# One batch boundary regrouped in a fused attention and mixer kernel: token products, transposes and one output tile in another order, q and k loaded one pair later

## The chip, the cores and the metric

The kernel runs on one core of one Trainium2 chip. The metric is device time in microseconds (us) of one execution; smaller is better. The kernel before has a median of 386.81 us over 4 runs (386.44 to 387.4).

## The reference

There are 8 batches of 12 heads, with 448 positions and a head dimension of 64. Cosine attention comes first: q and k are divided by their row norms, the scores are scaled by 1/tau, a softmax is taken, and the weights multiply v. The heads are joined to x of 448 by 768 for each batch. A mixer follows: one product along the tokens (448 to 256 and back), one along the channels (768 to 1536 and back), each with a ReLU between its two halves and a residual sum.

```python
q_n = q / (norm(q, axis=-1) + 1e-6);  k_n = k / (norm(k, axis=-1) + 1e-6)
attn = softmax(matmul(q_n, k_n.T) / tau)
x = matmul(attn, v)                                   # joined over heads: B, 448, 768
h = maximum(x.T @ w_tok1, 0.0) @ w_tok2
u = x + h.T
out = u + maximum(u @ w_ch1, 0.0) @ w_ch2
```

## The kernel before, in words

The work is cut into 48 pairs of heads, six to a batch; pair i belongs to batch i // 6. The order of all instructions is written out by hand: each engine runs its own queue in the order in which the source issues to it, and semaphores join the queues.

A pair passes through these steps, each a function of the source:

- `load_qk` and `load_v` (L121 and below) issue the loads on SyncE (SP). The q and k buffers hold 7 pairs, the v buffers 4.
- `square` (L237 on GpSimd, L235 on ScalarE) squares q and k, `sums` (L253, VectorE) adds them over the head dimension, `norms` (L264 and L265) takes the root on ScalarE as a logarithm and an exponential, and with `dve=True` (L261 and L262) adds the epsilon and inverts on VectorE. `scaled` (L276, GpSimd) multiplies q and k by the result. `tpose` (L300) turns both on TensorE, and VectorE copies them to `qk` (L302).
- `score(i, c)` (L323) makes the scores of a quarter of the keys in a two-bank PSUM tile, and ScalarE writes their exponentials to `pt` (L324). There are four quarters, c = 0 to 3.
- `pv` (L362) or `pv_wide` (L380) multiply them with v, and VectorE divides by the row sums (L365 and L366, or L383 and L384) to give `x`. `pv` takes two one-bank tiles, one a head; `pv_wide` takes one two-bank tile for both heads.
- `tok1` (L393, copy with ReLU L396) and `tok2` (L407, sum L410) are the token product; they give `u16`. `udma` (L416) turns `u16` into `ut` by a DMA transpose on SP. `upose` (L423, copy L424) does it on TensorE instead.

The channel product of a batch comes as a queue of units: 12 of `m_ch1` (`psG`, L433; ReLU L436 on ScalarE) and then those of `m_ch2` (`psF`, L449; sum L453 on VectorE). `refill(0)` fills the queue for batch 0 while pair 7 is in the main loop; a unit is taken out between the steps of a pair.

PSUM is split in two pools that rotate. Pool "b" has 2 buffers of one bank, pool "s" has 3 buffers of two banks. A new tile of "s" waits until the third tile before it is read out; a new one of "b" waits for the second before it. Scores and units called with `wide=True` take "s"; `tpose`, `tok1`, `tok2`, `upose` and `pv` take "b"; `pv_wide` takes "s".

Pairs 0 to 5 are staged in a first stretch without units. The end of batch 0 is written out around two iterations. In iteration i = 6 (`NPAIR`) TensorE is given the last two score quarters of pair 6, `tpose(7)`, `tok1(5)` and `tok2(4)`. In iteration i = 7 it is given three score quarters of pair 7, `tok2(5)`, `upose` of pairs 3 and 4 together, `upose` of pair 5, `pv` of pair 6, the first unit (`psG` number 0), the last score quarter of pair 7, `tpose(8)`, the second unit, `tok1(6)`, and then the scores of pair 8. Pairs 0, 1 and 2 were turned by DMA (`ut` parts 0, 1, 2).

On SP the loads of q and k of pair i + 6 are issued in iteration i. Each DMA on SP waits, before its issue, for the landing of the eighth DMA before it. From pair 12 on the keys' last 64 rows come as separate small loads (`kr`).

Of the kernel before, what the change touches and what calls it, by code (L numbers as in the profile page):

```python
# [22 lines left out]
def kernel(  # L23
# [20 lines left out]
    DT = D // 128  # L44
# [4 lines left out]
    NP_ALL = B * NPAIR  # L49
# [4 lines left out]
    DMA_T0 = 16  # L54
# [37 lines left out]
    pipe = {}  # L92
# [4 lines left out]
    def old(i):  # L97
        return i < OLD
# [22 lines left out]
    def load_qk(i):  # L121
        b, h0 = i // NPAIR, 2 * (i % NPAIR)
        n = i // HP
        half.setdefault(n, {})
        st = pipe[i] = {}
        st["q"] = qkv.tile([SC, QS, E], FP32, name=f"qf_{i}", tag="qf")
        nc.sync.dma_start(out=st["q"][:].rearrange("p (g c) e -> p g (c e)", g=2),
                          in_=q[b, h0:h0 + 2].rearrange("g (p c) e -> p g (c e)", c=NCH))
        st["k"] = load_rows(i, "k", k[b], 7)
        if not old(i) and "kr" not in half[n]:  # L130
            half[n]["kr"] = load_rest(i, "k", k[b])
# [107 lines left out]
    def squares(i):  # L239
        square(i, 0)  # L240
        square(i, 1)
# [45 lines left out]
    def scaled(i):  # L287
        scale(i, 0)
        scale(i, 1)
# [80 lines left out]
    def pv_wide(i):  # L370
        st = pipe[i]
        vt = vts[(i // HP) % NV]
        st["x"] = att.tile([128, 4, 128], FP16, name=f"x_{i}", tag="x", bufs=3)
        psO = ps2.tile([128, 2, 512], FP32, name=f"psO_{i}", tag="s")
        o = psO[:, :, 0:4 * (E + 2)].rearrange("p h (m e) -> p h m e", m=4)
        for hh in range(2):
            for m, lo in enumerate(windows(i // NPAIR)):
                for c in range(NCH):
                    at = (2 * c + hh) * S + lo
                    nc.tensor.matmul(o[:, hh, m, 0:E + 1], pts[i % 2][0:SC, at:at + 128],  # L380
                                     vt[0:SC, i % HP, NCH * hh + c, 0:E + 1], start=(c == 0), stop=(c == NCH - 1))
        rec = att.tile([128, 2, 4], FP32, name=f"rec_{i}", tag="rec2", bufs=2)
        nc.vector.reciprocal(out=rec[:], in_=o[:, :, :, E])  # L383
        nc.vector.tensor_tensor(out=st["x"][:].rearrange("p m (h e) -> p h m e", h=2), in0=o[:, :, :, 0:E],  # L384
                                in1=_bcast_free(rec[:], E), op=ALU.mult)
# [40 lines left out]
    def m_ch1(b, ct, wide):  # L426
        if b // 2 not in gts:
            gts[b // 2] = mix.tile([128, CT, 2 * S], FP16, name=f"gt_{b // 2}", tag="gt", bufs=1)
        gt = gts[b // 2]
        lo = 64 * (b % 2)  # L430
        psG = (ps2 if wide else ps).tile([128, 512], FP32, name=f"psG_{b}_{ct}", tag="s" if wide else "b")
        for dt in range(DT):
            nc.tensor.matmul(psG[:, 0:S], wc1t[:, dt, ct * 128:(ct + 1) * 128],  # L433
                             ut[b][:, dt].rearrange("p m s -> p (m s)")[:, lo:lo + S],
                             start=(dt == 0), stop=(dt == DT - 1))
        nc.scalar.activation(out=gt[:, ct, (b % 2) * S:(b % 2 + 1) * S], in_=psG[:, 0:S], func=AF.Relu)  # L436

    ost = {}
# [77 lines left out]
    with tc.manual_schedule():  # L516
        for i in range(3):
            load_qk(i)
        load_v(0)
        load_qk(3)  # L520
        load_v(1)
        load_qk(4)
        load_v(2)
        load_qk(5)
        load_v(3)
        nc.scalar.add_instruction(mybir.InstLoadActFuncSet(
            name=nc.get_next_instruction_name(), act_func_set_id=ACT_SET_LN_EXP,
            ins=[], outs=[]))
        weights_tok1()

        square(0, 1, act=True)
        square(0, 0, act=True)
        sums(0, 1, 2)
        norms(0, 1, 2)
        sums(0, 0, 1)
        norms(0, 1, 2, dve=True)
        norms(0, 0, 1)
        scale(0, 1, nc.vector)
        norms(0, 0, 1, dve=True)
        scale(0, 0)  # L540
        square(1, 1, act=True)
        square(1, 0, act=True)
        square(2, 1, act=True)
        warm(40, True)
        sums(1)
        norms(1)
        tpose(0, 1, 2)
        warm(3, True)
        tpose(0, 0, 1)
        warm(5, True)  # L550
        square(2, 0)
        weights_tok2()
        score(0, 0)
        score(0, 1)
        norms(1, dve=True)
        scale(1, 0)
        scale(1, 1, nc.vector)
        sums(2)
        norms(2)
        cast_v(0)  # L560
        score(0, 2)
        warm(8)
        tpose(1)
        score(0, 3)
        warm(6)
        norms(2, dve=True)
        square(3, 1, act=True)
        square(3, 0)
        load_v(4)
        load_qk(6)  # L570

        for i in range(1, NPAIR):
            if i == 1:
                scale(2, 0)
                scale(2, 1, nc.vector)
            else:
                scaled(i + 1)
                if i != 3:
                    weights_ch1(max(i - 3, 0))
            load_qk(i + 6)  # L580
            score(i, 0)
            score(i, 1)
            sums(i + 2)
            norms(i + 2)
            if i >= 2:
                tok1(i - 2)
            pv_wide(i - 1)
            norms(i + 2, dve=True)
            cast_v(i)
            square(i + 3, 0)  # L590
            if i == 1:
                warm(10)
            score(i, 2)
            score(i, 3)
            tpose(i + 1)
            if i >= 2:
                tok2(i - 2, pe=True)
            square(i + 3, 1, act=True)
            if i == 1:
                place_w2()  # L600
            load_v(i + 4)
            if 2 <= i < NPAIR - 1:
                udma(i - 2)

        i = NPAIR
        load_qk(i + 6)
        scaled(i + 1)
        score(i, 0)
        score(i, 1)
        sums(i + 2)  # L610
        norms(i + 2)
        tok1(i - 2)
        pv_wide(i - 1)
        norms(i + 2, dve=True)
        cast_v(i)
        load_v(i + 4)
        squares(i + 3)
        scaled(i + 2)
        weights_ch1(3)
        score(i, 2)  # L620
        score(i, 3)
        tpose(i + 1)
        tok1(i - 1)
        tok2(i - 2, pe=True)

        def side(i):
            if i + 6 < NP_ALL and i + 2 < DMA_T0:
                load_qk(i + 6)  # L630
            cast_v(i)
            if i + 3 < NP_ALL:
                squares(i + 3)
            if i in (8, 11):
                weights_ch2((i - 8) // 3)
            if i + 2 < NP_ALL:
                norms(i + 2)
                norms(i + 2, dve=True)
                scaled(i + 2)
                if i + 2 >= DMA_T0:  # L640
                    tpose_dma(i + 2)
            if i + 6 < NP_ALL and i + 2 >= DMA_T0:
                load_qk(i + 6)
            if i + 4 < NP_ALL:
                load_v(i + 4)

        for i in range(NPAIR + 1, NP_ALL):
            b, pj = i // NPAIR, i % NPAIR
            for c in range(KC):
                score(i, c)  # L650
            if i == NPAIR + 1:
                tok2(i - 2, pe=True)
                upose(i - 4, 2)
                upose(i - 2)
                sums(i + 2)
            pv_rest(i - 1)
            pv(i - 1, 0)
            pv(i - 1, 1)
            if i == NPAIR + 1:
                refill(0)  # L660
            elif pj == 2 and b > 1:
                refill(b - 1)
            side(i)
            fed[0] += fed[1]
            unit(True)
            if old(i):
                score(i, KC)
            else:
                score_rest(i)
            if i > NPAIR + 1:  # L670
                tok2(i - 2)
            if i + 1 < DMA_T0:
                tpose(i + 1)
            if due():
                unit(True)
            while due():
                unit()
            tok1(i - 1)
            if i + 3 < NP_ALL:
                sums(i + 3)  # L680
        last = NP_ALL - 1
        unit(True)
        pv_rest(last)
        pv(last, 0)
        pv(last, 1)
        unit(True)
        tok2(last - 1)
        unit(True)
        tok1(last)
        unit(True)  # L690
        unit(True)
        tok2(last)
        refill(B - 1)
        while queue:
            unit()
# [35 lines left out]
```

## Time and profile before

| what | value |
|---|---|
| median of 4 runs | 386.81 us (386.44 to 387.4) |
| the profiled execution's own time | 386.58 us |
| span inside it | 384.8 us |
| mean granted TensorE clock | 0.99 |
| TensorE matmuls busy | 372.3 us, 97% of the span |
| TensorE weight loads busy | 243.4 us, 63% |
| VectorE busy | 217.5 us, 57% |
| ScalarE busy | 226.6 us, 59% |
| GpSimd busy | 238.0 us, 62% |
| DMA | 64.21 MB, mean 167 GB/s |

The span is what the profile shows of the execution; the own time also holds what lies around it. PE is TensorE, PEld its weight loads, DVE VectorE, ACT ScalarE, POOL GpSimd, SPq the issues on SyncE. A timeline row has the start, the duration of the merged group, the engine, the line, the operation, and in brackets the idle time before it with what ended it. Ends of matmuls are modelled, so two groups on PE overlap a little in the rows.

### The profile page before, as it was taken

Reading aid. Unit: us, or ns where it says so; the run is one execution under the profiler, and the core shown is the slowest. Engines: PE = TensorE matmul, PEld = TensorE weight load, DVE = VectorE, ACT = ScalarE, POOL = GpSimd, SP = SyncE. Lnnn points to the kernel's source line nnn. Section 1 sums busy time; section 2 is a strip of 40 time slices with the busy share of each in tenths; the row PEclk is TensorE's granted clock in tenths of the full one; section 3 lists DMA queues with packets and bytes.
Section 4 is the critical chain, followed back from the end, with each engine's and each line's share of the span. In section 5 each row is a group of like instructions: output and inputs, shape, how many; then the busy total and the mean of one; then the engine's idle time right before and its main releaser. Section 6 shows DMA issues by size and latency. Waiting matters only on the chain.

```text
span 384.8 us, 10226 instructions
## 1 busy us (share of the span) xinstructions
PE 372.3 (97%) x4124; PEld 243.4 (63%) x4124; DVE 217.5 (57%) x520; ACT 226.6 (59%) x398; POOL 238.0 (62%) x383
## 2 busy tenths in 40 slices
PE   5989999999999999999999999999999999999995
PEld 4566666667657666667666666667666666665563
DVE  7789766777536674557545674656544673241032
ACT  5899687746665457855675456754675466601500
POOL 8999987978567577678567667768657733000000
PEclk9799999999999999999999999999999999999999
DMA  8999999994985888879995988978995755114023
GB/s 222 282 225 233 174 249 207 213 232 75 238 185 126 194 207 196 183 170 166 222 188 118 172 218 201 173 174 181 193 222 118 136 122 128 15 55 97 0 70 96
DMA packets 115423, 64.21 MB, mean 167 GB/s; under 512 B 71728, under 2 KB 111792, under 8 KB 115376
## 3 DMA queue, kind: packets, MB, share of 16 engines
q1 hardware_dynamic: 108944, 57.62, 68.9%
q0 software_dynamic: 5616, 5.21, 8.4%
q10 hardware_dynamic: 816, 0.73, 0.7%
q8 instruction: 32, 0.52, 0.6%
q14 instruction: 15, 0.12, 0.1%
HBM read 43.45 MB, written 11.01 MB: 142 GB/s over the span
## 4 chain that ended last, share of the span: by engine, by line
PE 90%; ACT 5%; DVE 2%; DMA 1%; issue 0%; POOL 0%; ACTq 0%; DVEq 0%
PE psF L449 28%; PE psG L433 28%; PE psO L362 10%; PE psS L323 8%; PE psU L407 5%; PE psR L393 5%; ACT pt L324 4%; PE psQ L330 2%; PE psO L345 1%; PE pst L300 1%; DMA qf<-in_q_dram 1%; ACT sq L235 1%; PE warm L314 1%; DVE ssq L253 0%; DVE u L410 0%
## 5 line engine op out<-in xcount | busy, mean ns | idle before, releaser
L324 ACT ACTIVATE pt<-psS 128x896 f16<-128x896 f32 (+1 forms) x156 | 132.6, 917 | 57.8 <-PE psS L323 57.8
L433 PE MATMUL psG<-ut,wc1t 128*128 128x448 f16 x576 | 116.6, 353 | 0.0
L449 PE MATMUL psF<-wc2t,gt 128*128 128x384 f16 (+2 forms) x684 | 116.2, 323 | 0.0
L276 POOL TENSOR_TENSOR kq<-kf,rn 128x384 f16<-128x384 f32 (+1 forms) x48 | 43.1, 897 | 75.4 <-DVE rn L262 70.6
L436 ACT ACTIVATE gt<-psG 128x448 f16<-128x448 f32 x96 | 51.9, 540 | 62.4 <-PE psG L433 62.4
L449 PEld LDWEIGHTS <-gt 128*128 128x128 f16 x684 | 64.1, 98 | 38.1
L433 PEld LDWEIGHTS <-wc1t 128*128 128x128 f16 x576 | 53.8, 98 | 44.3
L453 DVE TENSOR_TENSOR ost<-psF,u 128x384 f32<-128x384 f32 (+2 forms) x65 | 34.5, 531 | 57.1 <-PE psF L449 55.7
L253 DVE TENSOR_REDUCE ssq<-sq 128x15 f32<-128x960 f32 (+2 forms) x49 | 55.8, 1140 | 4.2 <-ACT sq L235 3.8
L396 DVE TENSOR_SCALAR rt<-psR 128x256 f16<-128x256 f32 x48 | 20.1, 420 | 59.5 <-PE psR L393 59.4
L276 POOL TENSOR_TENSOR kq<-qf,rn 112x512 f16<-112x512 f32 x45 | 47.0, 1043 | 3.0
L323 PE MATMUL psS<-qk 64*128 64x448 f16 x312 | 42.0, 362 | 2.7 <-DVE qk L302 2.4
L362 PE MATMUL psO<-vt,pt 128*128 128x65 f16 (+1 forms) x1056 | 40.4, 194 | 0.2 <-DVE ut L424 0.2
L237 POOL TENSOR_TENSOR sq<-qf 112x512 f32<-112x512 f32 x39 | 40.5, 1039 | 0.0
L237 POOL TENSOR_TENSOR sq<-kf 128x384 f32<-128x384 f32 (+1 forms) x46 | 40.1, 872 | 0.0
L362 PEld LDWEIGHTS <-pt 128*128 128x128 f16 (+1 forms) x1056 | 35.3, 97 | 4.0 <-PE psS L323 1.0
L366 DVE TENSOR_TENSOR x<-psO,rec 128x256 f16<-128x256 f32 x84 | 35.7, 425 | 2.9
L410 DVE TENSOR_TENSOR u<-psU,x 128x512 f16<-128x512 f32 x48 | 32.4, 674 | 4.7 <-PE psU L407 3.6
L393 PEld LDWEIGHTS <-w1t 128*128 128x128 f16 x384 | 25.0, 98 | 9.0 <-issue 2.3
L407 PEld LDWEIGHTS <-w2t 128*128 128x128 f16 x384 | 24.9, 98 | 7.8 <-issue 1.5
L393 PE MATMUL psR<-x,w1t 128*128 128x128 f16 x384 | 29.3, 220 | 0.4 <-DVE u L410 0.3
L407 PE MATMUL psU<-rt,w2t 128*128 128x128 f16 x384 | 29.4, 220 | 0.2 <-DVE qk L302 0.2
(54 smaller groups left out, 283.2 us busy)
## 6 DMA issues: line engine op xcount, KB each, us to landing
qf<-in_q_dram SPq DMA_DIRECT2D x48, 224.0 KB, 4.3
kf<-in_k_dram SPq DMA_DIRECT2D x36, 192.0 KB, 3.7
vf<-in_v_dram SPq DMA_DIRECT2D x36, 192.0 KB, 3.7
vf<-in_v_dram SPq DMA_DIRECT2D x12, 224.0 KB, 7.1
out_dram<-ost SPq DMA_DIRECT2D x8, 336.0 KB, 3.5
wc1t<-in_moe_w_ch_dram POOLq DMA_DIRECT2D x4, 576.0 KB, 9.5
wc2t<-in_moe_w_ch_dram POOLq DMA_DIRECT2D x2, 1152.0 KB, 13.7
out_dram<-ost SPq DMA_DIRECT2D x8, 288.0 KB, 3.3
```

What stands on the lines that cost most here:

```text
L237: nc.gpsimd.tensor_mul(out=dst, in0=src, in1=src)
L253: nc.vector.tensor_reduce(out=st["ssq"][0:n, sl], in_=st["sq"][0:n, sl], axis=AXX.X, op=ALU.add)
L276: eng.tensor_tensor(out=kq[0:p, a, 0:n].rearrange("p c g e -> p g c e"), in0=st["kq"[a]][:].rearrange("p (g c) e -> p g c e", g=2), in1=_b ...
L323: nc.tensor.matmul(psS[:, hh, 0:S], qk[hb, c * n:c * n + 128], qm[hb], start=True, stop=True)
L324: nc.scalar.activation(out=pts[i % 2][0:n, 2 * S * c:2 * S * (c + 1)].rearrange("p (h s) -> p h s", h=2), in_=psS[0:n, :, 0:S], func=AF.Ex ...
L362: nc.tensor.matmul(psO[:, m, 0:E + 1], pts[i % 2][0:n, at:at + 128], vt[0:n, i % HP, nch * hh + c, 0:E + 1], start=(old(i) and c == 0), st ...
L366: nc.vector.tensor_tensor(out=st["x"][:, :, hh * E:(hh + 1) * E], in0=psO[:, :, 0:E], in1=_bcast_free(rec[:], E), op=ALU.mult)
L393: nc.tensor.matmul(psR[:, tt], w1t[:, w1[m], tt * 128:(tt + 1) * 128], st["x"][:, m], start=(m == 0), stop=(m == 3))
L407: nc.tensor.matmul(psU[:, m], w2t[:, tt, lo:lo + 128], st["rt"][:, tt], start=(tt == 0), stop=(tt == TT - 1))
L433: nc.tensor.matmul(psG[:, 0:S], wc1t[:, dt, ct * 128:(ct + 1) * 128], ut[b][:, dt].rearrange("p m s -> p (m s)")[:, lo:lo + S], start=(dt ...
L436: nc.scalar.activation(out=gt[:, ct, (b % 2) * S:(b % 2 + 1) * S], in_=psG[:, 0:S], func=AF.Relu)
L449: nc.tensor.matmul(psF[:, 0:hi - lo], gt[:, ct, at:at + 128], wc2t[:, ct, lo:hi], start=(ct == 0), stop=(ct == CT - 1))
```

## The change

Five edits, all but the last at the end of batch 0:

1. Iteration 6: `tok2(4)` goes ahead of `tpose(7)`, which stands ahead of `tok1(5)`; the VectorE half of `norms(8)` goes from right after the division of pair 5 to behind `tpose(7)`, and `scaled(8)` with it. `scaled(8)` and `weights_ch1(3)` keep their place behind `squares(9)` on GpSimd.
2. Iteration 7: `upose` of pairs 3 and 4 goes ahead of `tok2(5)`; pair 6's output is made by `pv_wide` between `tok2(5)` and `upose(5)`; its division (now a function of its own, `x_wide`) comes after `upose(5)`, and `sums(9)` after that. Before, `sums(9)` stood ahead of pair 6's output.
3. `pv_wide` is split in two, matmuls and division; every other caller calls both in a row.
4. The first unit of batch 0 adds its six parts in the order 0, 1, 3, 4, 2, 5.
5. From pair 9 on the loads of q and k are issued five pairs ahead in place of six: none in iteration 3, then pair i + 5 in iteration i.

```diff
         i = NPAIR
-        load_qk(i + 6)
+        load_qk(i + 5)
         scaled(i + 1)
 ...
         pv_wide(i - 1)
-        norms(i + 2, dve=True)
+        x_wide(i - 1)
         cast_v(i)
         load_v(i + 4)
         squares(i + 3)
+        score(i, 2)
+        score(i, 3)
+        tok2(i - 2, pe=True)
+        tpose(i + 1)
+        norms(i + 2, dve=True)
         scaled(i + 2)
         weights_ch1(3)
-        score(i, 2)
-        score(i, 3)
-        tpose(i + 1)
         tok1(i - 1)
-        tok2(i - 2, pe=True)
 ...
             if i == NPAIR + 1:
+                upose(i - 4, 2)
                 tok2(i - 2, pe=True)
-                upose(i - 4, 2)
+                pv_wide(i - 1)
                 upose(i - 2)
+                x_wide(i - 1)
                 sums(i + 2)
-            pv_rest(i - 1)
-            pv(i - 1, 0)
-            pv(i - 1, 1)
+            else:
+                pv_rest(i - 1)
+                pv(i - 1, 0)
+                pv(i - 1, 1)
 ...
+        dts = (0, 1, 3, 4, 2, 5) if (b, ct) == (0, 0) else range(DT)
+        for n, dt in enumerate(dts):
 ...
-            load_qk(i + 6)
+            if i != 3:
+                load_qk(i + (6 if i < 3 else 5))
 ...
         def side(i):
-            if i + 6 < NP_ALL and i + 2 < DMA_T0:
-                load_qk(i + 6)
+            if i + 5 < NP_ALL and i + 2 < DMA_T0:
+                load_qk(i + 5)
 ...
-            if i + 6 < NP_ALL and i + 2 >= DMA_T0:
-                load_qk(i + 6)
+            if i + 5 < NP_ALL and i + 2 >= DMA_T0:
+                load_qk(i + 5)
```

More of the change, by code (lines that the diff above doesn't have):

```diff
@@ L381, in pv_wide, with x_wide @@
                                      vt[0:SC, i % HP, NCH * hh + c, 0:E + 1], start=(c == 0), stop=(c == NCH - 1))
+        st["o"] = o
+    def x_wide(i):
+        st = pipe[i]
+        o = st["o"]
         rec = att.tile([128, 2, 4], FP32, name=f"rec_{i}", tag="rec2", bufs=2)
@@ L431, in m_ch1 @@
         psG = (ps2 if wide else ps).tile([128, 512], FP32, name=f"psG_{b}_{ct}", tag="s" if wide else "b")
-        for dt in range(DT):
+        dts = (0, 1, 3, 4, 2, 5) if (b, ct) == (0, 0) else range(DT)
+        for n, dt in enumerate(dts):
             nc.tensor.matmul(psG[:, 0:S], wc1t[:, dt, ct * 128:(ct + 1) * 128],
                              ut[b][:, dt].rearrange("p m s -> p (m s)")[:, lo:lo + S],
-                             start=(dt == 0), stop=(dt == DT - 1))
+                             start=(n == 0), stop=(n == DT - 1))
         nc.scalar.activation(out=gt[:, ct, (b % 2) * S:(b % 2 + 1) * S], in_=psG[:, 0:S], func=AF.Relu)
@@ L651 @@
             if i == NPAIR + 1:
+                upose(i - 4, 2)
                 tok2(i - 2, pe=True)
-                upose(i - 4, 2)
+                pv_wide(i - 1)
                 upose(i - 2)
+                x_wide(i - 1)
                 sums(i + 2)
-            pv_rest(i - 1)
-            pv(i - 1, 0)
-            pv(i - 1, 1)
+            else:
+                pv_rest(i - 1)
+                pv(i - 1, 0)
+                pv(i - 1, 1)
             if i == NPAIR + 1:
```

## The prediction

> **What bounds the kernel now.** I read the page first, for the shares, the clock and the chain that ended last. Then came the chain and the timeline of all engines between 36 and 50 us, where the end of batch 0 lies, then the waits, and the landing times of single loads.
>
> ```profile
> span 384.8 us, 10226 instructions
> PE 372.3 (97%) x4124; PEld 243.4 (63%) x4124; DVE 217.5 (57%) x520; ACT 226.6 (59%) x398; POOL 238.0 (62%) x383
> ...
> PE 90%; ACT 5%; DVE 2%; DMA 1%; issue 0%; POOL 0%; ACTq 0%; DVEq 0%
> ```
>
> TensorE carries 90% of the chain. The ScalarE share is almost all from 18 to 36 us, where four exponentials, one square and the norm of each pair fill a period of 4.2 us. From 44 us on TensorE goes from group to group with hardly a wait. So whatever the change wins or loses is the shift of TensorE's queue at the point where that steady stretch begins. The timeline there:
>
> ```profile
> 38.13 0.69 DVE L384 TENSOR_TENSOR x<-psO,rec 128x512 f16<-128x512 f32 x1
> 38.29 0.57 PE L300 MATMUL pst<-id,kq 112*128 112x112 f16 x8
> 39.73 0.61 PE L407 MATMUL psU<-rt,w2t 128*128 128x128 f16 x8 [0.23 <-DVE qk L302]
> 40.27 0.74 PE L323 MATMUL psS<-qk 64*128 64x448 f16 x6
> 40.94 0.62 PE L407 MATMUL psU<-rt,w2t 128*128 128x128 f16 x8
> 41.60 0.69 DVE L410 TENSOR_TENSOR u<-psU,x 128x512 f16<-128x512 f32 x1 [0.54 <-PE psU L407]
> 42.35 0.40 PE L423 MATMUL psT<-id,u 128*128 128x128 f16 x4 [0.34 <-DVE u L410]
> 42.95 1.19 PE L362 MATMUL psO<-vt,pt 112*128 112x65 f16 x32 [0.20 <-DVE ut L424]
> 43.14 1.21 DVE L253 TENSOR_REDUCE ssq<-sq 112x16 f32<-112x1024 f32 x1
> 43.98 1.30 PE L433 MATMUL psG<-ut,wc1t 128*128 128x448 f16 x6
> 44.38 0.31 ACT L264 ACTIVATE rn<-ssq,tiny 112x16 f32<-112x16 f32 x1 [1.18 <-DVE ssq L253]
> 45.31 0.54 ACT L436 ACTIVATE gt<-psG 128x448 f16<-128x448 f32 x1 [0.38 <-PE psG L433]
> 45.75 0.91 ACT L324 ACTIVATE pt<-psS 112x896 f16<-112x896 f32 x1
> 47.24 0.54 ACT L436 ACTIVATE gt<-psG 128x448 f16<-128x448 f32 x1 [0.58 <-PE psG L433]
> 47.59 0.74 PE L323 MATMUL psS<-qk 64*128 64x448 f16 x6
> 48.26 1.19 PE L362 MATMUL psO<-vt,pt 112*128 112x65 f16 x32
> ```
>
> The reader is to see two things. TensorE stands still three times (0.23, 0.34 and 0.20 us) for VectorE's copies and sums, and that is what the change regroups. And ScalarE's logarithm for pair 9 (44.38) waits 1.18 us for `ssq` of pair 9 on VectorE, ahead of the first ReLU (45.31), the last exponential of pair 7 (45.75) and the second ReLU (47.24). In the rows each engine starts its work in the order of the source.
>
> **The change, part by part.** A group's start to the next group's start is taken from the rows: 0.46 us for eight products of 128, 0.40 for a pair's eight transposes, 0.67 for three score quarters, 1.03 for `psO`, 1.14 for `psG`, 0.54 from a product of eight to scores. A reader on VectorE starts 0.64 after the start of a group of eight (39.73 to 40.37). TensorE follows 0.06 after VectorE's end.
>
> *Tokens of pair 4 first (edit 1).* `psU` of pair 4 takes the place at 38.29; its sum starts at 38.93, as VectorE is just done with the division (38.13 + 0.69), and ends at 39.62. `tpose(7)` runs at 38.75, but its copy stands behind that sum: 38.93 + 0.61 = 39.54, done at 40.10 (before 39.11 + 0.56 = 39.67). `psR` of pair 5 needs the bank of pair 4's `psU`: 39.68, against 38.88. The scores of pair 7 follow at 39.68 + 0.54 = 40.22, against 40.27. So this edit moves 0.46 us of work out of the way and pays it back in waits; ScalarE gets its scores 0.05 us sooner. The norm of pair 8 comes after the copy, at 40.6 in place of 39.2; GpSimd's `scaled(8)` has the squares of pair 9 ahead of it until 40.07, so it starts at 40.55 in place of 40.04, and the `wc1t` load, the cast and `squares(10)` behind it slide by 0.5. `tpose(8)` wants that result only at 44.6, and it is there at 42.6: no cost.
>
> *Transposes and pair 6's output (edit 2).* `psT` of pairs 3 and 4 at 40.22 + 0.67 = 40.89, `psU` of pair 5 at 41.35, `psO` of pair 6 at 41.81 to 42.84. VectorE copies the first `psT` from 41.53, then adds pair 5 from 42.13 to 42.82 (0.60 after that copy's start, by 42.21 to 42.81). `upose(5)` runs at 42.88, as `psO` now covers its wait, and the first `psG` at 43.11 in place of 43.98. That is a gain of **0.87 us**. Its buffer (the third tile back is a score quarter whose exponential ends near 42.4) is free. In the new order the transpose by DMA of pair 2 is its fifth operand, wanted at 43.9: before it landed at 31.93 + 11.2 = 43.1 with two more loads ahead of it. No cost. Two divisions of 0.60 (44.26 to 45.36 with both reciprocals) become one of 0.84: VectorE saves 0.26 us once.
>
> *Where the gain goes.* After `psG`, the rows give the last quarter of pair 7 at 44.34, `tpose(8)` 44.63, the second `psG` 45.04, `psR` of pair 6 46.18, and the scores of pair 8 could start at 46.72, against 47.59. But `sums(9)` now stands behind `upose(5)`'s copy (43.32), the reciprocal (43.65) and the division (43.88) on VectorE. It runs from 44.49 to 45.70, against 43.14 to 44.35: **1.35 us later**. Queued behind it are the logarithm on ScalarE (45.73), the exponential (0.34 later, 46.07), the first ReLU (0.12 later, 46.19, in place of 45.31), the last exponential of pair 7 (0.44 later, 46.63 to 47.54) and the second ReLU (0.80 later, 47.43 to 47.97). The three score tiles of pair 8 take just the buffers that these last three read out, in this order. On VectorE the inverse for pair 9 (46.32) and the copy of `tpose(8)` behind it are done at 47.41. So the quarters of pair 8 start at about 47.5, 47.6 and 48.03; before, the third was at 47.59 + 0.39 = 47.98. The sum is -0.87 + 0.92 = **+0.05 us**. TensorE then enters the steady stretch where it did. ScalarE's exponentials of pair 8 start at 47.87 against 47.99 and `ssq` of pair 10 at 47.55 against 48.03, so nothing else arrives late.
>
> Does a ready ReLU wait behind a logarithm that isn't? In the row at 44.38 ScalarE waited 1.18 us, but nothing behind it was ready, so the row alone leaves it open. The Trainium skill ("PSUM — Partial Sum Buffer", section "Engine vs sequencer instructions") states that the queues of ScalarE, VectorE and GpSimd are strictly first in, first out. By that rule the 0.87 us are lost as above; if the ReLUs could pass, the sum would stay near -0.87.
>
> *Loads one pair later (edit 5).* Counts and bytes are the same. Keys of pair 10 take the place on SP that those of pair 11 had, behind the third DMA transpose: issue at 33.79. The same loads stand ahead of their end as ahead of that transpose's end before, so 43.1 is the near bound; the row of that very place took 13.4 us, so 47.2 is the far one. I take the near one, as two loads fewer are in the queue. GpSimd asks at 43.9, squares for 2.0 us, and VectorE asks for the result at 47.55. So up to about 45.5 lateness costs nothing. At 47.2 `ssq` runs from 49.3, pair 7's first division ends at 51.1, and `psU` of pair 6, which wants its bank at 50.9, waits **0.3 us**. Price taken 0, far end 0.3. Later loads: keys of pair 20 would be issued with those of 21 (102.5), take 3.7 us by the median of their line, and are wanted at 108.15; the sum over squares comes 3.8 us after these end (76.85 to 80.64). Covered. I price edits 3 and 4 at nothing: 4 only moves an operand that would land late.
>
> **The rivals.**
>
> *The gain stays (faster).* It holds if pair 9's logarithm starts by 44.9 or does not hold the score buffers. For it: 0.77 us of the gain is idle time that the rows really show. Against it: eight rows in one chain, all in source order. The time would be 386.81 - 0.87 = 385.94.
>
> *Keys land late (slower).* Place: keys of pairs 10 and 11, through GpSimd's squares and VectorE's `ssq`. It decides from a landing of pair 10 at 46.9; each us beyond that costs one. For it: between 38 and 42 us the DMA moved 52 GB/s by the busy table, against 243 in the next 6 us, and the load issued at 37.12 took 15.9 us. With that latency pair 10 lands at 49.7: 2.8 us late, 389.6. Against it: that place follows more loads than pair 10 has ahead of it.
>
> **How the numbers follow.** The profiled execution took 386.58 us (span 384.8 and 1.8 around it), 0.23 below the median of 386.81. With +0.05 it would be 386.63, and the median **386.9**. Its own range is 386.5 to 387.4 (hand-overs in the chain off by 0.3 us in sum, plus 0.3 for late keys). A measurement of this kernel can tell about 0.2%, 0.77 us, from no change. The forecast has 0.6 and all of it lies within that. The first rival has 0.2, the second 0.2. The range reaches below the first rival, 385.8, and into the second up to 388.2, which leaves about 0.15 outside.
>
> **What would show it.** Right: the first `psG` at about 43.1 without a wait of 0.3 us on TensorE before it; the logarithm after it at 45.7; scores of pair 8 in three pieces to 48.0, with waits on ScalarE. Wrong: scores of pair 8 near 46.7 (first rival); `sq` of pair 10 on GpSimd waiting for a DMA beyond 46 (second); or idle TensorE after 50 us, which no step here has.

## The result, and the profile after

The changed kernel has a median of 387.33 us over 43 runs (386.51 to 391.08); the kernel before, on the same chips, 386.50 us over 64 (385.92 to 392.07). The ratio is 1.0028, with an interval of 1.0018 to 1.0037. The change makes the kernel 0.8 us slower; 386.9 was forecast, in a range of 385.8 to 388.2.

The profiled execution of the changed kernel took 390.5 us, far above that median: it shows a loss that most executions have in part or not at all. First its page: the span, the engines, and the chain that ended last.

```profile
span 388.4 us, 10208 instructions
...
PE 373.8 (96%) x4124; PEld 243.8 (63%) x4124; DVE 217.1 (56%) x518; ACT 226.3 (58%) x398; POOL 237.9 (61%) x383
...
PE 85%; DMA 7%; DVE 3%; POOL 2%; ACT 1%; issue 1%; SPq 0%; POOLq 0%; ACTq 0%; DVEq 0%
```

The chain has a new part: 7% in transfers, where it was 1%. Of these, 4% is a single load of keys; another 2% is a load of weights from 10.2 to 18.5 us. The end of batch 0, from the timeline of the same execution:

```profile
38.22 0.62 PE L412 MATMUL psU<-rt,w2t 128*128 128x128 f16 x8
39.62 0.61 PE L398 MATMUL psR<-x,w1t 128*128 128x128 f16 x8 [0.39 <-DVE u L415]
40.16 0.74 PE L323 MATMUL psS<-qk 64*128 64x448 f16 x6
41.73 1.18 PE L380 MATMUL psO<-vt,pt 112*128 112x65 f16 x32
43.07 1.30 PE L439 MATMUL psG<-ut,wc1t 128*128 128x448 f16 x6
44.45 1.21 DVE L253 TENSOR_REDUCE ssq<-sq 112x16 f32<-112x1024 f32 x1
45.70 0.31 ACT L264 ACTIVATE rn<-ssq,tiny 112x16 f32<-112x16 f32 x1 [2.61 <-DVE ssq L253]
46.16 0.53 ACT L442 ACTIVATE gt<-psG 128x448 f16<-128x448 f32 x1
46.51 0.25 DVE L262 RECIPROCAL rn<-rn 112x16 f32<-112x16 f32 x1
46.68 0.56 DVE L302 COPY qk<-pst 128x896 f16<-128x896 f16 x1
47.30 1.04 PE L323 MATMUL psS<-qk 64*128 64x448 f16 x6 [0.55 <-DVE qk L302]
47.38 0.55 ACT L442 ACTIVATE gt<-psG 128x448 f16<-128x448 f32 x1
47.98 0.09 PEld L323 LDWEIGHTS <-qk 64*128 64x128 f16 x1 [0.34 <-issue]
48.27 1.19 PE L362 MATMUL psO<-vt,pt 112*128 112x65 f16 x32
```

The reader is to see that the forecast chain of waits is there: the first `psG` at 43.07 (43.11 forecast, 43.98 before), the logarithm of pair 9 at 45.70 (45.73), the first ReLU, by now long ready, at 46.16 (46.19), and `psO` of pair 7 at 48.27 (48.31 forecast, 48.26 before). TensorE waits twice on the way. The first scores of pair 8 wait 0.55 us for VectorE's copy of `tpose(8)` (done at 47.24), which stood behind the inverse for pair 9. The last of the three quarters starts only at 47.98, just after ScalarE's second ReLU has ended (47.38 + 0.55). The 0.9 us won are lost again within 5 us.

What follows was forecast as the slower rival only. The timeline goes on:

```profile
48.70 1.04 POOL L237 TENSOR_TENSOR sq<-kf 112x512 f32<-112x512 f32 x1 [4.63 <-DMA kf<-in_k_dram]
50.77 1.22 DVE L253 TENSOR_REDUCE ssq<-sq 112x16 f32<-112x1024 f32 x1 [3.21 <-POOL sq L237]
52.60 0.62 PE L412 MATMUL psU<-rt,w2t 128*128 128x128 f16 x8 [1.70 <-DVE x L366]
```

The chain of waits of the same execution gives the load behind it (start, duration):

```profile
33.72 14.85 DMA kf<-in_k_dram
```

Keys of pair 10 land at 48.56. GpSimd's squares wait for them, VectorE's sum over the squares waits for those, pair 7's two divisions stand behind that sum in VectorE's queue, and TensorE waits 1.70 us for the first of them. Then the granted clock falls. In the busy table by stretches the columns are the stretch, its length, the busy time of PE, PEld, DVE, ACT and POOL with their instructions, the granted clock, the DMA share and GB/s:

```profile
53.00:54.00 1.00, 0.98 (x14) 0.66 (x12) 0.96 (x5) 0.82 (x2) 0.83 (x2) 1.00 0.95 213
54.00:55.00 1.00, 1.00 (x4) 0.40 (x3) 0.54 (x2) 0.00 (x0) 1.00 (x2) 0.55 0.98 218
55.00:56.00 1.00, 1.00 (x4) 0.46 (x3) 0.00 (x0) 0.37 (x1) 1.00 (x2) 0.50 1.06 276
56.00:57.00 1.00, 1.00 (x4) 0.42 (x3) 0.00 (x0) 0.17 (x1) 0.98 (x2) 0.50 0.86 199
57.00:58.00 1.00, 1.00 (x11) 0.61 (x9) 0.00 (x0) 0.22 (x1) 1.00 (x2) 0.74 1.06 118
```

TensorE counts as busy from 54 us on, but has half its clock for 3.4 us: the twelve products of the two units that start there take 4.12 us, and 2.44 in a second trace of the same kernel (e12 below). A busy share of 1.00 hides this; the column of the granted clock shows it.

**Two distances** read from the timelines sort all the traces. The first runs from the first scores of pair 0 to the third `psG` and holds the whole reordered part. The second runs from the third `psG` to the last `psF` and holds the steady stretch, where only late data and the clock can lose time. The last column is own time less span, as the median over a kernel's runs.

| kernel | first scores to third `psG` | third `psG` to last `psF` | keys of pair 10 land | outside the span |
|---|---|---|---|---|
| before | 49.29 - 10.21 = 39.08 | 380.45 - 49.29 = 331.16 | 37.97 | 1.77 |
| after | 49.30 - 10.16 = 39.14 | 384.07 - 49.30 = 334.77 | 48.56 | 2.13 |
| after, second trace (e12) | 49.11 - 10.10 = 39.01 | 380.39 - 49.11 = 331.28 | 46.57 | 2.11 |
| after with memsets (e9) | 49.11 - 10.24 = 38.87 | 381.73 - 49.11 = 332.62 | 47.90 | 2.14 |

So the new order costs between -0.2 and +0.1 us in these traces, the steady stretch is 0.1 to 3.6 us longer, and some 0.36 us more lie outside the profiled span, whatever the execution.

### The profile page after: what moved, and what is told of

Same layout as the page of the kernel before. It is cut to its first block, busy times and chain, and to the rows that moved or that the text cites. A ratio compares the mean times of both kernels' runs of the same rounds, so it can differ in the third digit from the quotient of the medians.

```text
span 388.4 us, 10208 instructions
## 1 busy us (share of the span) xinstructions
PE 373.8 (96%) x4124; PEld 243.8 (63%) x4124; DVE 217.1 (56%) x518; ACT 226.3 (58%) x398; POOL 237.9 (61%) x383
## 4 chain that ended last, share of the span: by engine, by line
PE 85%; DMA 7%; DVE 3%; POOL 2%; ACT 1%; issue 1%; SPq 0%; POOLq 0%; ACTq 0%; DVEq 0%
PE psF L455 28%; PE psG L439 28%; PE psO L362 9%; PE psS L323 7%; PE psU L412 5%; PE psR L398 5%; DMA kf<-in_k_dram 4%; DMA w2n<-in_moe_w_tok_dram 2%; PE psQ L330 2%; PE psO L345 1%; DVE ssq L253 1%; DMA qf<-in_q_dram 1%; POOL kq L276 1%; POOL sq L237 1%; PE pst L300 1%
## 5 line engine op out<-in xcount | busy, mean ns | idle before, releaser
L439 PE MATMUL psG<-ut,wc1t 128*128 128x448 f16 x576 | 118.3, 356 | 0.0
L276 POOL TENSOR_TENSOR kq<-qf,rn 112x512 f16<-112x512 f32 x45 | 46.9, 1043 | 3.0
L362 PE MATMUL psO<-vt,pt 128*128 128x65 f16 (+1 forms) x1024 | 39.2, 194 | 0.0
L366 DVE TENSOR_TENSOR x<-psO,rec 128x256 f16<-128x256 f32 x82 | 34.8, 425 | 2.8
L362 PEld LDWEIGHTS <-pt 128*128 128x128 f16 (+1 forms) x1024 | 34.2, 97 | 3.5 <-issue 0.9
```

Source lines behind the costliest of these rows:

```text
L276: eng.tensor_tensor(out=kq[0:p, a, 0:n].rearrange("p c g e -> p g c e"), in0=st["kq"[a]][:].rearrange("p (g c) e -> p g c e", g=2), in1=_b ...
L362: nc.tensor.matmul(psO[:, m, 0:E + 1], pts[i % 2][0:n, at:at + 128], vt[0:n, i % HP, nch * hh + c, 0:E + 1], start=(old(i) and c == 0), st ...
L366: nc.vector.tensor_tensor(out=st["x"][:, :, hh * E:(hh + 1) * E], in0=psO[:, :, 0:E], in1=_bcast_free(rec[:], E), op=ALU.mult)
```

## The experiments

My theory from these traces was this. (A) The gain at the first `psG` is lost to the wait for pair 9's norm, as forecast. (B) The loss comes from keys that land late behind a stretch, between 37 and 42 us in the traces of before and after, in which the DMA queues hardly move; a transpose by DMA is in flight then. The rivals: the new order costs by itself; the later loads cost throughout the steady stretch; the loss is not in the profiled span at all.

**e1: edits 1 to 4 alone, loads six pairs ahead.**

```diff
-            if i != 3:
-                load_qk(i + (6 if i < 3 else 5))
+            load_qk(i + 6)
 ...
-        load_qk(i + 5)
+        load_qk(i + 6)
```
(and `i + 6` at the two places in `side`)

> The changed kernel with loads of q and k six pairs ahead again (edits 1 to 4 alone). If the whole loss comes from the late keys of pair 10, this one takes the time of the kernel before, +0.05 us (386.5 to 386.6), TensorE starts the product of pair 7 with v at 48.3, and the squares of pair 10 wait for no load. If the new order itself costs, it stays 0.8 to 1.1 us above the kernel before.

Measured: 386.77 us against 386.53, ratio 1.0012 (0.9986 to 1.0038). The distances are 39.01 and 331.13: order and steady stretch cost nothing. 2.12 us lie outside the span against 1.77, which is more than the difference of the medians (0.24). Two of 12 executions took 390.5 and 391.0. In this trace the second unit starts 0.5 late, since TensorE waits inside the first one, for the third transpose by DMA (`ut` of pair 2), which landed at 44.28:

```profile
42.96 0.92 PE L439 MATMUL psG<-ut,wc1t 128*128 128x448 f16 x4
44.33 0.54 PE L439 MATMUL psG<-ut,wc1t 128*128 128x448 f16 x2 [0.45 <-DMA ut<-u]
```

The wait does not show in the third `psG`, because the last scores of pair 8 wait for ScalarE anyway.

**e2: edit 5 alone, on the kernel before.**

```diff
-            load_qk(i + 6)
+            if i != 3:
+                load_qk(i + (6 if i < 3 else 5))
 ...
-        load_qk(i + 6)
+        load_qk(i + 5)
```
(and `i + 5` in `side`)

> The kernel before with loads of q and k five pairs ahead (edit 5 alone). If late keys are the cause, it loses about what the whole change loses, 0.8 to 1.1 us, keys of pair 10 land near 47 to 49 us, and in a profile GpSimd's squares of pair 10 wait for them. If the new order is the cause, it takes the time of the kernel before.

Measured: 386.65 us against 386.53, ratio 1.0005 (0.9988 to 1.0023); distances 38.91 and 331.13; 1.78 outside the span. Keys of pair 10 landed at 46.06, 12.35 us after their issue, in time for this execution. Four of 12 took 387.6 to 388.6, the other eight 386.2 to 386.7. Neither half of the change by itself can be told from no change. Nor do the two intervals rule out that one of them costs most of the 0.8 us (0.2%): they reach to 0.38% and 0.23%.

**e3: the new order, six ahead up to iteration 13, five ahead from 15 on.** It asks whether the shorter lead costs in the steady stretch.

```diff
-            if i + 5 < NP_ALL and i + 2 >= DMA_T0:
+            if i > 14 and i + 5 < NP_ALL:
                 load_qk(i + 5)
```
(six ahead at the three earlier places)

> The changed kernel with loads six pairs ahead up to iteration 13 and five ahead from iteration 15. If five ahead costs only where the DMA queue is deep (up to some 60 us), it equals the run with six ahead everywhere, within 0.1 us. If it costs in the steady stretch, it is slower than that by some tenths, with GpSimd's squares waiting for loads.

Measured: 387.06 us, ratio 1.0023 (0.9996 to 1.005), distances 39.21 and 331.13. The steady stretch is the same to 0.03 us with loads five ahead, so the shorter lead costs nothing there. The median is not explained by that, though it lies 0.5 us above that of the kernel before: single executions reach 392.0 (391.0 in e1, which has the same order and the same loads up to iteration 13). What makes these stays open.

**e5: the changed kernel, with the sum over pair 10's squares behind the division of pair 7.** If late keys hold TensorE by that sum alone, they can't now.

```diff
+            if i == NPAIR + 2:
+                sums(i + 2)
 ...
-            if i + 3 < NP_ALL:
+            if i + 3 < NP_ALL and i != NPAIR + 1:
                 sums(i + 3)
```

> The changed kernel, loads five ahead, but the sum over the squares of pair 10 placed behind the division of pair 7 on VectorE. If the late keys act through VectorE's queue, they still land at 47 to 49 us, but TensorE's wait of 1.7 us before the token product of pair 6 goes, and so does most of the loss: within 0.3 us of the kernel before. If they act through GpSimd or ScalarE, the loss stays at 0.8 to 1.1 us.

Measured: 387.10 us (386.64 to 387.62), ratio 1.0007 (0.9995 to 1.0018). In its profiled execution the keys came early (42.76), so the trace doesn't show the cover at work. The times do: none of 12 executions lies above 387.62, while 19 of the changed kernel's 43 do. Were the two alike, the 19 highest of the 55 times would all fall to the changed kernel with a chance of 0.3%. The price is 0.17 in the second distance (331.30), and 2.1 stay outside the span. So the times agree with late keys that act through this one place in VectorE's queue, the place where the trace of the changed kernel shows TensorE's wait.

**e4: loads six ahead, pair 9's norm behind the transposes of pair 8.** It takes away what makes the ready ReLU wait.

```diff
-            if i + 2 < NP_ALL:
+            if i + 2 < NP_ALL and i != NPAIR + 1:
                 norms(i + 2)
 ...
                 tpose(i + 1)
+            if i == NPAIR + 1:
+                norms(i + 2)
+                norms(i + 2, dve=True)
+                scaled(i + 2)
```

> Edits 1 to 4, loads six pairs ahead as before, and pair 9's norm moved: its logarithm and exponential on ScalarE, its inverse on VectorE and its scaling on GpSimd stand behind the transposes of pair 8 instead of ahead of the first ReLU. If the gain of 0.87 us at the first psG is lost because a ReLU that is ready waits behind pair 9's logarithm (my theory): the first ReLU starts at about 44.4, the scores of pair 8 at about 46.7 without waiting for ScalarE, psO of pair 7 at about 47.4 (48.27 after the change), span 383.8 to 384.2, time 385.9 to 386.3. Where the third DMA transpose lands after 43.8, as with the first six-ahead kernel, half of that is lost again. If the gain is lost elsewhere (the order itself costs, or score buffers are held by something else): psO of pair 7 stays at 48.2 or later and the time at 386.7 or more.

Measured: 386.86 us, ratio 0.9994 (0.9978 to 1.0009); the four fastest executions took 385.81 to 386.45, the slowest 392.9. The median missed what was expected. The trace says why:

```profile
43.21 0.92 PE L439 MATMUL psG<-ut,wc1t 128*128 128x448 f16 x4
44.98 0.54 PE L439 MATMUL psG<-ut,wc1t 128*128 128x448 f16 x2 [0.86 <-DMA ut<-u]
47.83 0.74 PE L323 MATMUL psS<-qk 64*128 64x448 f16 x6
48.51 1.19 PE L362 MATMUL psO<-vt,pt 112*128 112x65 f16 x32
```

The scores of pair 8 no longer wait, neither for VectorE's copy nor for ScalarE (0.74 long in one piece, no bracket; 1.04 with 0.55 of waiting before it after the change). But the third transpose by DMA lands at 44.94, and the wait for it, 0.86 us here and hidden in e1, now shows: the first distance is 39.33.

**e7: the changed kernel, with pair 2 turned on TensorE as well.** Only two transposes by DMA are left.

```diff
-            if 2 <= i < NPAIR - 1:
+            if 2 <= i < NPAIR - 2:
                 udma(i - 2)
 ...
+                upose(i - 5)
                 upose(i - 4, 2)
```
(and natural order of the parts in the first unit)

> The changed kernel with pair 2 turned on TensorE, so that only two transposes by DMA are left, and parts in natural order in the first unit. If the third DMA transpose makes the stretch between 37 and 42 us in which the queues hardly move, and that stretch makes the keys of pair 10 late (my theory): the DMA rate of 38 to 42 us is near the 150 GB/s of its neighbours or more, keys of pair 10 land by 42, and no execution is above 388. The price is four products and a copy more: 0.4 to 0.7 us, span about 385.3, time 387.2 to 387.5. If the loads themselves crowd the queues (rival): a rate near 50 GB/s stays somewhere in 36 to 44, keys of pair 10 land at 43 to 49 as after the change, and single executions stay 3 us longer.

Measured: 387.42 us, ratio 1.0016 (0.9999 to 1.0033), distances 39.47 and 331.12. The busy table from 38 to 42 us, the kernel after first, then this one:

```profile
38.00:42.00 4.00, 3.61 (x57) 2.73 (x57) 3.07 (x8) 3.33 (x6) 4.00 (x6) 1.00 1.43 75
```
```profile
38.00:42.00 4.00, 3.55 (x55) 2.75 (x54) 3.30 (x8) 3.36 (x5) 3.61 (x4) 1.00 1.12 268
```

The DMA share is no lower in the first (1.43 against 1.12), but the transfers move 75 GB/s with the third transpose in flight and 268 without it. One trace could be chance, so here are the GB/s of the busy table for each microsecond from 36 to 45, for every kernel:

| kernel | third transpose by DMA | GB/s, microsecond by microsecond from 36 |
|---|---|---|
| before | yes | 322 132 29 48 54 78 225 244 255 |
| after | yes | 232 226 88 72 66 74 133 249 254 |
| after, second trace (e12) | yes | 236 235 211 97 201 201 175 243 328 |
| e9 | yes | 231 219 26 46 50 53 178 243 244 |
| e1 | yes | 231 293 239 242 219 147 40 215 304 |
| e3 | yes | 237 234 242 230 184 132 173 232 328 |
| e2 | yes | 237 148 53 45 41 120 270 248 253 |
| e5 | yes | 237 60 275 231 238 238 298 381 317 |
| e4 | yes | 254 225 239 244 233 244 253 62 261 |
| e7 | no | 292 242 229 241 268 335 288 298 224 |
| e8 | no | 255 228 230 246 233 242 241 338 307 |
| e10 (below) | no | 242 230 258 231 244 237 338 305 300 |
| e11 (below) | no | 300 229 236 244 264 323 278 271 246 |

Every trace with it has a dip (below 150 GB/s), of one to five microseconds and at varying places; none without it falls below 224 there. The dips are not the third transpose's alone. From 26 to 36 us, where the first two are in flight, the four kernels without the third have short ones too: in their lowest microsecond they move 40 (e7), 113 (e8), 39 (e10) and 27 GB/s (e11). And the keys follow the landing of the third transpose: it lands at 38.62 in e5, 42.10 in e2, 43.34 in e9, 43.52 and 43.69 in the two traces of the changed kernel, and the keys of pair 10, issued behind it, 2.9 to 5.0 us later.

In e7, keys of pair 10 land at 40.02: they are issued 2.8 us sooner (30.90), as the transpose no longer stands ahead of them on SP, and fly 9.1 us in place of 14.85. The price of the four products is 0.33 in the first distance. Three of 12 executions still took 388.1 to 388.5, which was not expected; the kernel before has such executions too.

**e8: e4 and e7 together, loads six ahead.** The edits are those of e4 and of e7.

> Edits 1 to 4 with loads six ahead, pair 9's norm behind the transposes of pair 8, and pair 2 turned on TensorE. If both theories hold: 0.87 gained, 0.4 to 0.7 paid for the fourth pair of transposes, nothing lost to a late third transpose; span 384.2 to 384.6, time 386.2 to 386.7, no execution above 388. If the stretch in the DMA does not come from the transpose, the spread of single executions stays as with the first six-ahead kernel (up to 391).

Measured: 386.65 us (386.22 to 387.45), ratio 0.9995 (0.9976 to 1.0014), distances 38.99 and 331.15. None of the 12 executions lies at 390 or above. From the first `psG` to `psO` of pair 7 it takes 48.40 - 44.12 = 4.28 us, against 48.27 - 43.07 = 5.20 in the changed kernel. The difference, 0.92, is the sum that the prediction had put on the wait for pair 9's logarithm. Turning pair 2 here takes up most of it.

**e10 and e11: the same, with pair 2 turned at 36 us, where TensorE has time.** Loads six ahead in e10 and five ahead in e11.

```diff
         score(i, 0)
+        upose(i - 4)
         score(i, 1)
 ...
-                upose(i - 5)
                 upose(i - 4, 2)
```
(iteration 6; the second hunk against e8)

> Edits 1 to 4 with loads six ahead, pair 9's norm behind the transposes of pair 8, and pair 2 turned on TensorE right behind the first score quarter of pair 6 (35.6 us), where TensorE otherwise waits for ScalarE; two transposes by DMA are left. If both theories hold (the gain of 0.87 is lost by the wait for pair 9's logarithm; the third transpose by DMA makes the operand or the keys late): the cost of the four products there is 0 to 0.3, psO of pair 7 starts at 47.4 to 47.7 against 48.27 after the change, span 384.0 to 384.3, time 386.0 to 386.4 with 2.1 outside the span (385.7 to 386.1 with 1.8), no execution above 388. If the gain is bound by something else on VectorE there: first psG at 43.6 or later and the time as with the same at the later place (386.65).

> The same with the loads of q and k five ahead, as in the change. If the late keys came from the third transpose by DMA: keys of pair 10 land by 43, and time and spread are as with six ahead, 386.0 to 386.4. If the short lead by itself makes them late: keys at 45 or later, TensorE waits before pair 6's second token product again (now wanted about 0.8 us earlier), single executions above 388.

Measured: e10 386.46 us (386.07 to 386.85), ratio 0.9986 (0.9974 to 0.9999); e11 386.52 us (386.18 to 387.06), ratio 0.9995 (0.9987 to 1.0004); the kernel before, measured beside them, 386.70. Both medians lie a little above what was expected (up to 386.4). Both have 38.35 in the first distance, 0.73 less than before, and 331.14 and 331.13 in the second. The timeline of e11:

```profile
43.10 1.30 PE L439 MATMUL psG<-ut,wc1t 128*128 128x448 f16 x6
45.72 0.31 ACT L264 ACTIVATE rn<-ssq,tiny 112x16 f32<-112x16 f32 x1
46.37 0.54 ACT L442 ACTIVATE gt<-psG 128x448 f16<-128x448 f32 x1
46.71 0.74 PE L323 MATMUL psS<-qk 64*128 64x448 f16 x6
47.38 1.19 PE L362 MATMUL psO<-vt,pt 112*128 112x65 f16 x32
48.41 1.30 PE L439 MATMUL psG<-ut,wc1t 128*128 128x448 f16 x6
```

The logarithm comes as late as after the change (45.72), but no ReLU and no copy stands behind it any more: the first ReLU starts at 44.43, the scores of pair 8 have no wait, and `psO` of pair 7 starts 0.89 us sooner. With the lead of five pairs kept, keys of pair 10 are issued at 31.19 and land at 39.24. So the third transpose made them late, and not the lead alone. The interval of e10 lies just below 1 and that of e11 holds it, so a gain over the kernel before is barely told, and it is less than the first distance gives: 0.73 won there, 0.35 lost outside the span.

**e9: the changed kernel with six short memsets more on VectorE at the start.**

```diff
         nc.vector.memset(ne[:, :, 1], EPS_NORM)
+        nc.vector.memset(ne[:, :, 1], EPS_NORM)
+        nc.vector.memset(ne[:, :, 1], EPS_NORM)
```

> The changed kernel with six short memsets more on VectorE at the start (the three that set the epsilon are each done three times); nothing else. It asks whether the time outside the span (1.8 us before, 2.1 after the change) goes by the number of VectorE's instructions. If it does: own time less span 1.8 or another value than 2.13, and the time 386.9 to 387.0. If it belongs to the placing of the work and not to counts: 2.13 again, time 387.3.

Measured: 387.48 us, ratio 1.003 (1.0007 to 1.0053), and 2.14 outside the span. It doesn't go by the number of VectorE's instructions. The trace is worth more than the answer, since here the keys are late without the loss of clock:

```profile
48.03 1.04 POOL L239 TENSOR_TENSOR sq<-kf 112x512 f32<-112x512 f32 x1 [4.19 <-DMA kf<-in_k_dram]
50.11 1.22 DVE L255 TENSOR_REDUCE ssq<-sq 112x16 f32<-112x1024 f32 x1 [2.74 <-POOL sq L239]
51.94 0.62 PE L414 MATMUL psU<-rt,w2t 128*128 128x128 f16 x8 [1.23 <-DVE x L368]
```

After this wait of 1.23 us the granted clock stays at 1.00 in every stretch, and the second distance is 1.5 us longer, against 3.6 with the wait of 1.70.

**e12: the changed kernel a second time.**

> The changed kernel itself a second time, for a second trace. If the wait of 1.7 us and the half clock behind it belong to some executions only (my theory, as most times lie near 387): the order chain repeats (first psG 43.1, psO of pair 7 48.3), keys of pair 10 land somewhere between 42 and 49, and span is 384.5 to 386. If they belong to the order of the changed kernel: 388.4 again.

Measured: 386.81 us, span 384.7. The same order chain and late keys without a loss:

```profile
46.70 1.04 POOL L237 TENSOR_TENSOR sq<-kf 112x512 f32<-112x512 f32 x1 [2.87 <-DMA kf<-in_k_dram]
48.77 1.22 DVE L253 TENSOR_REDUCE ssq<-sq 112x16 f32<-112x1024 f32 x1 [1.40 <-POOL sq L237]
50.64 0.62 PE L412 MATMUL psU<-rt,w2t 128*128 128x128 f16 x8
```

GpSimd waits for the transfer here too, but TensorE's product stands without a bracket. Half of the changed kernel's 44 recorded spans (one more than the times above) lie from 384.4 to 385.2 and four from 388.2 to 389.0; both traces belong to one kernel.

## Why the prediction was right, and where it was not

**The order (edits 1 to 4): right.** +0.05 was forecast for the start of the steady stretch. By the first distance it was +0.06 in the first trace, -0.07 in the second, -0.07 in e1, +0.13 in e3 and -0.21 in e9. Each step is where it was put: the gain of 0.9 at the first `psG`, the loss of the same size between the first unit and the scores of pair 8. Moving pair 9's norm out of the way (e8, e11) gives the gain back, so this cause is shown. These kernels move its ScalarE, VectorE and GpSimd parts together, so no run parts the two queues; the rows of the changed kernel do. With VectorE's copy as the only wait, the three quarters would have run from 47.30 and `psO` would have come 0.67 later, at 47.97 (an estimate from the rows); ScalarE's second ReLU put it at 48.27. It also answers the question that the rows of before left open: a ready ReLU does stand behind a logarithm that isn't ready. The Trainium skill's first-in, first-out rule ("PSUM — Partial Sum Buffer", section "Engine vs sequencer instructions") agrees with this case: in the changed kernel the ReLU started at 46.16, though the products of its `psG` were done by 44.4 (43.07 + 1.30); in e11, with no logarithm ahead of it, it started at 44.43.

**The faster rival: its condition named rightly.** "It holds if pair 9's logarithm ... does not hold the score buffers" is what e10 and e11 make true. Of the 0.87 they keep 0.73, which leaves 0.14 for pair 2's transposes.

**The late keys: the mechanism and its slope were right, the value taken was not.** Two of the prediction's own signs of being wrong are there: GpSimd's squares of pair 10 wait for a load beyond 46 in both traces of the changed kernel (to 48.70 and 46.70), and in the first TensorE stands idle after 50 us. The landing was bounded by 43.1 and 47.2, and I took the near end, "as two loads fewer are in the queue". The five traces with that place of the load and three transposes by DMA show 42.76, 46.06, 46.57, 47.90 and 48.56: four near the far end, two of them beyond it. The far end should have been taken, or both weighed. What was argued for the near end counted loads, where it was the transpose in flight that counted; the prediction had seen its 52 GB/s and hadn't asked what made them. From 46.9 on each us late was to cost one. At 47.90 that gives 1.0, and TensorE waited 1.23; at 48.56 it gives 1.7, and TensorE waited 1.70; at 46.57 it gives nothing, and there was no wait. The term priced at 0 cost 0 to 3.6 in single executions. In the median the span grew by about 0.5 (384.7 to 385.2). That late keys are all of this is not shown: e11, where they come early and the norm is moved, has 384.4 and e1, with the longer lead, 384.65, but e3, with the same lead as e1 at this place, has 385.25.

**The clock: not foreseen.** Of the 3.6 us more in the profiled execution 1.70 are the wait itself, and 3.41 us at half clock make another 1.7; some 0.2 is left over.

**Outside the span: not foreseen.** I took 1.8 us as fixed. It is fixed for a program, but not across programs: 1.77 to 1.82 for before, e2 and e3; 2.09 to 2.15 for the changed kernel and the other eight. That is 0.36 of the 0.83 us lost. It follows neither the order (e1 against e3) nor the lead (e2 against e11) nor the count on VectorE (e9). Its cause stays open.

Put together: 386.50, the median of before over many runs, plus 0.47 in the span and 0.36 outside it, is 387.33. The forecast of no gain held for the reason given. The loss that it didn't see lies where it put zero: in the time outside the span, and, as far as the single executions tell, in late keys. That the number came within 0.43 us owes something to luck: the forecast added 0.05 to a median of four runs, 386.81, which lay 0.31 above that of 64. From 386.50 the same sum gives 386.55, and 0.78 us are missing.

## What to carry to other kernels

Before a load is given a shorter lead, look at which slow transfer it falls behind, and take the longest flight that the trace shows for that place; it is not the number of loads ahead that decides. A gain on one engine lasts only as far as the next hand-over to an engine that works in order: 0.9 us won on TensorE was lost to one pair's norm in the queues of ScalarE and VectorE, and came back when that norm was moved too. Where the next gain is of a few tenths of a microsecond, compare spans as well as times.

## What the runs showed of the hardware

A single wait of 1.70 us on TensorE (50.9 to 52.6) was followed, 1.5 us later, by 3.41 us at half the granted clock; one of 1.23 us (e9) was not. The Trainium skill ("TensorE: Matmul & The Clock Gate", section "What's actually happening") speaks of at least one idle window of about 3.4 us before the clock falls. The length of the slow spell agrees with such a window, but the idle time that came before it here was half of that, and the measurement decides. Where the waits lie can be worked out from the steps of the granted clock. After the change it was full from 13.15 to 54.11 us, which is twelve times 3.41. The last of these twelve stretches, from 50.69 on, holds the whole wait, with TensorE busy for 1.71 of its 3.42 us. Counted the same way from the step at 12.69, the wait of e9 lies whole in the stretch from 50.23 to 53.65, with 2.17 us busy. So half a stretch of idleness was followed by half the clock here and 1.25 us was not; with one trace each, the limit between them isn't known.

With the third transpose by DMA, of a 128 by 512 tile, comes a stretch in which the other transfers hardly move, at 26 to 148 GB/s where 224 to 338 are seen without it. It lasted one microsecond in some traces and four or five in others, even with the same program (five after the change, one in e12). What sets its length stays open; no run here was made to tell.
